# Converting two weight matrices beside the mix steps, and moving the products of zeros behind the first gates

## The chip, the core and the metric

One core of a Trainium2 chip. Its engines are the Tensor engine (PE; its weight loads are shown apart as PEld), the Vector engine (DVE), the Scalar engine (ACT), the GpSimd engine (POOL) and the Sync engine (SP), whose queue issues every transfer of this kernel. The metric is the device time of one execution in microseconds (us). Before the change it is 402.92 us, the median of three runs (402.27 to 406.24).

## What is computed

Three layers in a row on float32 data, 4 batches, 768 positions, 320 channels (8 heads of 40):

```python
# 1. a gated linear recurrence over the positions t, for each head
m_new = max(f[t] + m, i[t]);  f_s = exp(f[t] + m - m_new);  i_s = exp(i[t] - m_new)
C = f_s * C + i_s * outer(v[t], k[t]);  n = f_s * n + i_s * k[t]
x[t] = sigmoid(o[t]) * (C @ q[t]) / max(abs(n . q[t]), 1)
# 2. theta = x @ w_theta; token mixing with two 768 x 768 matrices; a ReLU layer
u = x + w_tok_r @ (x * cos(theta)) + w_tok_i @ (x * sin(theta));  x = u + relu(u @ w_ch)
# 3. a causal convolution of 5 taps (conv_w) as a gate, then two matrices
out = (sigmoid(conv(x)) * (x @ w_val)) @ w_out
```

## The kernel before

The recurrence is computed in blocks, as 12 units of attention (`attend`, L761; four batches, three units of 256 positions each). A unit has a matrix of weights `W` (`weigh`: sums of gate terms in two banks of PSUM, exponentiated by ACT), scores (`scores`: q times k in the same two banks; DVE multiplies them into `W`), the products with v (`numer`, into banks 2 and 3), a carried state (`carry`), the products of q with it (`inter`, into banks 4 and 5), and `finish`, in which DVE reads banks 4, 5, 2 and 3 into `num_m`, divides and writes the result for layer 2. The gates come first (`gates`, L692): scans and exponentials on 32 partitions. `parts` (L707) splits the two rows of gate terms, `G` and `c`, into three bf16 parts each; `weigh` multiplies these.

Layer 2 has 24 steps of mixing (`mix`, L908), six for each pair of batches and half of the positions. A step makes 30 products of 128x128 by 128x384, six into each of the banks 0 to 4. It needs a pair `z` (from `theta`, L824: transposes, products with `w_theta`, sine and cosine) and a pair `w` (from `weight`, L887: in the first twelve steps a token matrix is loaded and converted from 64-bit words, in two buffers `wt_m` used in turn). After six steps `f_u`, `f_ch`, `f_val` and `f_out` (L972 to L1035) do the rest of layers 2 and 3 for that half, between the steps of the next. The banks 0 to 4 are those that attention uses, so the mix begins when the last unit's `finish` has read them.

The small weight matrices come as 64-bit words too. `cv_piece` (L620) loads a third of one (128x320), scales it on ACT (`cv_scale`), puts the bits together with one TENSOR_SCALAR and two SCALAR_TENSOR_TENSOR on DVE (`cv_bits`), copies the high part on ACT and subtracts the low part on DVE or POOL. There are 13 pieces: three each of `w_theta`, `w_ch`, `w_val` and `w_out`, and one of the convolution's weights. They go through two buffers in `xT_m[1]`.

The code does not issue instructions as it runs. Each call is recorded, in program order, by a planner (`Plan`; hence nearly every instruction of the profile has the helper's line, L65), which gives the Tensor engine's steps due times in that order, gives the others the times by which they are needed, and then lists each engine's instructions by its own model of costs. `any2` means DVE or POOL, `copy` means ACT or DVE, as the planner chooses. Each engine then runs its list strictly in order. In the loop below one unit of attention is followed by one piece and by a step (for the negative numbers, of loads, weights and thetas alone):

```python
    for d in range(-1, NG):
        attend(d)
        for piece in [next(todo, None)]:
            if piece:
                cv_piece(*piece)
        step(d - NG)
    stage[0] = 1
    for n in range(NS):
        step(n)
```

At the start, seven products of zeros (`WARM`, L30 and L674) keep the Tensor engine busy while the gates are computed.

Of the kernel before, what the change touches and what calls it, by code (L numbers as in the profile page):

```python
# [7 lines left out]
F32 = mybir.dt.float32  # L8
# [3 lines left out]
I64 = mybir.dt.int64  # L12
# [6 lines left out]
DM = H * D  # L19
# [7 lines left out]
XB = 5  # L27
AHEAD = 3
CVL = (2,)
WARM = 7  # L30
RFIRST = (1,)
GATES = (0, 2, 4)
U = L // 2
NU2 = S // U
FAR = -32768.0
# [35 lines left out]
class Plan:  # L71
# [9 lines left out]
    HOP, TABLE, HOLD = 0.15, 1.3, 5.0  # L81
    WINDOW, PHASE, WARM, COLD = 3.413, 0.6, 0.85, 0.45
    BLOCK, FETCH = 127, 3.6
# [111 lines left out]
    def order(self, aim=None):  # L195
# [27 lines left out]
        def array(n, t):  # L223
# [5 lines left out]
            while todo:  # L229
                some = min(todo, self.BLOCK - used)  # L230
                left = some * each
                while left > 1e-6:
                    w = int((t + self.PHASE + 1e-6) / self.WINDOW)
                    for _ in range(window, w):
                        share, worked = worked / self.WINDOW, 0.0
                        slow = share < (self.WARM if slow else self.COLD)
                    window = w
# [104 lines left out]
def tile_kernel(ctx, tc, qT, kT, kt, v1, og, ig, fg, w_th, w_ch, w_val, w_out, cw, wtok,  # L342
                ident, selL, selR, selG, out):
    plan = Plan(tc.nc)
    act, dve, pool, pe, sp = plan.act, plan.dve, plan.pool, plan.pe, plan.sp
# [42 lines left out]
    k_m = [words(8 * GC * L, f"k_m{i}") for i in range(2)]  # L388
    q_m = words(12 * GC * L, "q_m", place="q")
    xT_m = [words(5 * TH, f"xT_m{i}") for i in range(2)]  # L390
    th_m = words(7 * DM, "th_m")
    num_m = words(2 * TH, "num_m", place="sr")
# [10 lines left out]
    bank = [ps.tile([128, 512], F32, name=f"bank{i}") for i in range(8)]  # L403
# [215 lines left out]

    def cv_piece(nm, src, k_):  # L620
        t = turn("cv", 2)
        raw = xT_m[1][:, t * 2 * DM:(t + 1) * 2 * DM].bitcast(I64)
        v = xT_m[1][:, (4 + t) * DM:(5 + t) * DM]
        if nm == "cw":
            raw, v = raw[:, 0:15], cw_sb.rearrange("p j t -> p (j t)")
        sp.dma_start(out=raw, in_=src if nm == "cw" else src[:, k_ * DM:(k_ + 1) * DM])
        cv_scale(raw, v)
        cv_bits(raw, v)
        if nm == "cw":
            return  # L630
        if nm == "th":
            w0, w1 = (t[:, k_] for t in w_t)
            if k_ == 2:
                pool.memset(w0[64:], 0.0)
                pool.memset(w1[0:64], 0.0)
                dve.tensor_scalar(out=w0[0:64], in0=v[0:64], scalar1=INV2PI, scalar2=None, op0=ALU.mult)
                act.activation(out=w1[64:, 64:], in_=v[64:, 0:256], func=AF.Copy, scale=INV2PI)
                act.activation(out=w1[64:, 0:64], in_=v[64:, 256:], func=AF.Copy, scale=INV2PI)
                return
            dve.tensor_scalar(out=w0, in0=v, scalar1=INV2PI, scalar2=None, op0=ALU.mult)  # L640
            act.activation(out=w1[:, 64:], in_=w0[:, 0:256], func=AF.Copy)
            act.activation(out=w1[:, 0:64], in_=w0[:, 256:], func=AF.Copy)
            return
        hi, lo = wsp[nm]
        act.activation(out=hi[:, k_, 0:DM], in_=v, func=AF.Copy)
        n = DM if nm == "out" else 256
        any2.tensor_tensor(out=lo[:, k_], in0=v[:, 0:n], in1=hi[:, k_, 0:n].bitcast(F32),
                           op=ALU.subtract)
        if n < DM:
            any2.tensor_tensor(out=hi[:, k_, DM:384], in0=v[:, 256:DM],  # L650
                               in1=hi[:, k_, 256:DM].bitcast(F32), op=ALU.subtract)

    pieces = [(nm, src, k_) for nm, src in (("th", w_th), ("ch", w_ch), ("val", w_val),
                                            ("out", w_out)) for k_ in range(3)]
# [11 lines left out]
    G_bf, c_bf = (b_m[:, n * S // 2:(n + 1) * S // 2].bitcast(BF16) for n in range(2))  # L666
# [4 lines left out]
    sp.dma_start(out=i_sb, in_=ig)  # L671
    sp.dma_start(out=id_sb, in_=ident)
    dve.memset(num_m[:, 0:256], 0.0)
    for n in range(WARM):  # L674
        pe.matmul(bank[6 + n % 2][:, 0:256], num_m[:, 0:128], num_m[:, 0:256], start=True, stop=True)
    dve.memset(m_sb[:, 0:1], NEG)
    dve.memset(r_sb, 1.0)
    dve.memset(r_sb.rearrange("p (c l) -> p c l", l=U)[:, :, 0:1], 0.0)
# [13 lines left out]
    def gates(c0, c1):  # L692
        n, a, e = c1 - c0, c0 * L, c1 * L
        m0, m1 = m_sb[:, a:e], m_sb[:, 1 + a:1 + e]
        g, G, c_, w, r, e_ = (t[:, a:e] for t in (g_sb, G_sb, i_sb, w_sb, r_sb, e_sb))
        eng = any2 if c0 else dve
        dve.tensor_tensor_scan(out=m1, data0=f_sb[:, a:e], data1=c_,
                               initial=m_sb[:, a:a + 1] if c0 else NEG, op0=ALU.add, op1=ALU.max)
        eng.tensor_tensor(out=g, in0=f_sb[:, a:e], in1=m0, op=ALU.add)
        eng.tensor_tensor(out=g, in0=g, in1=m1, op=ALU.subtract)  # L700
        dve.tensor_scalar(out=g, in0=g, scalar1=GMIN, scalar2=None, op0=ALU.max)
        if c0 == 0:
            dve.memset(g_sb[:, 0:1], 0.0)
        dve.tensor_tensor_scan(out=G, data0=r, data1=g, initial=0.0, op0=ALU.mult, op1=ALU.add)
        d, mid = d_sb[:, 0:e - a], mid_sb[:, 0:e - a]

        def parts(src, out):  # L707
            copy.copy(out[0:BH, a:e], src)
            eng.tensor_tensor(out=d, in0=src, in1=out[0:BH, a:e], op=ALU.subtract)
            copy.copy(mid, d)  # L710
            copy.copy(out[BH:2 * BH, a:e], mid)
            eng.tensor_tensor(out=d, in0=d, in1=mid, op=ALU.subtract)
            copy.copy(out[2 * BH:3 * BH, a:e], d)

        eng.tensor_tensor(out=c_, in0=c_, in1=m1, op=ALU.subtract)
        eng.tensor_tensor(out=c_, in0=c_, in1=G, op=ALU.subtract)
        parts(G, G_bf)
        parts(c_, c_bf)
        G3, w3, c3 = (t.rearrange("p (c l) -> p c l", l=U) for t in (G, w, c_))
        eng.tensor_tensor(out=w3, in0=c3, in1=G3[:, :, U - 1:U].to_broadcast([BH, 2 * n, U]), op=ALU.add)  # L720
        act.activation(out=w, in_=w, func=AF.Exp)
        e4, G4 = e_.rearrange("p (g u i l) -> p g u i l", i=2, u=2, l=U), G.rearrange(
            "p (g i u l) -> p g u i l", i=2, u=2, l=U)
        for u in range(2):
            act.activation(out=e4[:, :, u], in_=G4[:, :, u], func=AF.Exp)
        tv = bank[5 + turn("g", 3)][:, 0:n * BH].rearrange("p (c h) -> p c h", c=n)
        with plan.joined():
            for c in range(n):
                pe.transpose(tv[:, c, :], w[:, c * L:(c + 1) * L], id_sb[0:BH, 0:BH])
        copy.copy(ew[:, c0:c1, :], tv)  # L730
        tv = bank[5 + turn("g", 3)][:, 0:n * BH].rearrange("p (g u h) -> p g u h", u=2, h=BH)
        with plan.joined():
            for g_ in range(n // 2):
                for u in range(2):
                    o = (2 * g_ + u) * L
                    pe.transpose(tv[:, g_, u], e_[:, o:o + L], id_sb[0:BH, 0:BH])
        copy.copy(ee[:, c0 // 2:c1 // 2], tv)
# [352 lines left out]
            theta(*first_use[n])  # L1090

    parts = []
    todo = iter(pieces)
    for d in range(-1, NG):
        attend(d)
        for piece in [next(todo, None)]:
# [1 line left out]
                cv_piece(*piece)  # L1098
        step(d - NG)
    stage[0] = 1  # L1100
    for n in range(NS):
        step(n)
    stage[0] = 2

    parts.append(part[:])
# [83 lines left out]
```

## Time and profile before

| | |
|---|---|
| median of three runs | 402.92 us (402.27 to 406.24) |
| the profiled execution | 401.29 us, of which 399.6 us are the span from the first to the last instruction |
| PE busy | 359.5 us (90% of the span), mean granted clock 0.936 |
| DVE busy | 324.9 us (81%) |
| ACT busy | 222.0 us (56%) |
| POOL busy | 82.8 us (21%) |

A busy PE is not one at its peak, since products are pipelined. The granted clock is a share of full speed: 0.5 is 1.2 GHz and 1.0 is 2.4 GHz. Engines run side by side, so an engine's idle time matters only where the chain of waits runs through it. "issue" in a wait is time for which the profile shows no reason.

### The profile page before, as it was taken

Reading aid. Unit: us, or ns where it says so; the run is one execution under the profiler, and the core shown is the slowest. Engines: PE = TensorE matmul, PEld = TensorE weight load, DVE = VectorE, ACT = ScalarE, POOL = GpSimd, SP = SyncE. Lnnn points to the kernel's source line nnn. Section 1 sums busy time; section 2 is a strip of 40 time slices with the busy share of each in tenths; the row PEclk is TensorE's granted clock in tenths of the full one; section 3 lists DMA queues with packets and bytes.
Section 4 is the critical chain, followed back from the end, with each engine's and each line's share of the span. In section 5 each row is a group of like instructions: output and inputs, shape, how many; then the busy total and the mean of one; then the engine's idle time right before and its main releaser. Section 6 shows DMA issues by size and latency. Waiting matters only on the chain.

```text
span 399.6 us, 11339 instructions
## 1 busy us (share of the span) xinstructions
PE 359.5 (90%) x4724; PEld 327.0 (82%) x4724; DVE 324.9 (81%) x632; ACT 222.0 (56%) x388; POOL 82.8 (21%) x102
## 2 busy tenths in 40 slices
PE   6877777888969679899999999999999999999996
PEld 4556656576757457799999999999999999999996
DVE  7958977978888899798978998769997759468990
ACT  3562636061866968576534278975697332335563
POOL 7212233345164300000002014023011010213320
PEclk9565889896999878999999999999999999999999
DMA  6977866887788666787875254620410420000204
GB/s 165 292 200 219 270 177 182 226 253 213 201 288 243 180 228 204 243 281 276 287 256 197 100 170 146 214 79 2 157 52 29 157 80 0 2 0 2 99 34 164
DMA packets 29299, 65.62 MB, mean 164 GB/s; under 512 B 5216, under 2 KB 14592, under 8 KB 29248
## 3 DMA queue, kind: packets, MB, share of 16 engines
q1 hardware_dynamic: 29248, 64.90, 51.2%
q8 instruction: 37, 0.61, 0.6%
q14 instruction: 14, 0.11, 0.1%
HBM read 47.58 MB, written 17.30 MB: 162 GB/s over the span
## 4 chain that ended last, share of the span: by engine, by line
PE 71%; DVE 16%; issue 6%; ACT 5%; DMA 1%; SPq 0%; DVEq 0%; ACTq 0%
PE bank L65 71%; DVE k_m L65 5%; DVE th_m L65 2%; ACT th_m L65 2%; DVE r_b L65 2%; DVE xT_m L65 1%; DVE W L65 1%; DVE num_m L65 1%; ACT L65 1%; DVE g_m L65 1%; DVE z L65 1%; DMA g_m<-in_ig_dram 1%; DVE wt_m L65 0%; ACT xT_m L65 0%; ACT xs_hi L65 0%
## 5 line engine op out<-in xcount | busy, mean ns | idle before, releaser
L65 PE MATMUL bank<-wt_m,z 128*128 128x384 f32 x480 | 89.1, 342 | 4.1 <-DVE num_m L65 2.8
L65 PEld LDWEIGHTS bank<-wt_m,z 128*128 128x128 f32 x480 | 83.9, 190 | 5.9 <-ACT xT_m L65 3.1
L65 PE MATMUL bank<-w_r,z 128*128 128x384 f32 x240 | 43.2, 337 | 0.0
L65 PEld LDWEIGHTS bank<-w_r,z 128*128 128x128 f32 x240 | 41.5, 188 | 0.0
L65 DVE SCALAR_TENSOR_TENSOR k_m<-k_m,cw_sb,k_m 128x384 f32<-128x384 f32 (+1 forms) x52 | 40.3, 811 | 0.4
L65 ACT ACTIVATE W<-bank 128x512 f32<-128x512 f32 x24 | 14.2, 597 | 31.5 <-PE bank L65 31.3
L65 POOL TENSOR_TENSOR hl_f<-k_m,hl_f 128x768 fp32r<-128x768 f32 x4 | 8.3, 2083 | 97.1 <-ACT hl_f L65 97.1
L65 ACT ACT_TABLE_LOAD x21 | 26.9, 1283 | 1.4 <-DVE th_m L65 1.0
L65 ACT ACTIVATE th_m<-bank,magic 128x320 f32<-128x320 f32 x24 | 12.6, 524 | 23.1 <-PE bank L65 15.1
L65 DVE TENSOR_TENSOR f_m<-f_m,bank 104x164 f32<-104x164 f32 (+1 forms) x36 | 15.1, 420 | 12.4 <-PE bank L65 8.3
L65 PE MATMUL bank<-r_b,W 64*64 64x41 f32 x768 | 16.8, 242 | 8.5 <-issue 5.5
L65 PE MATMUL bank<-w_t,xT_m 128*128 128x320 f32 x72 | 23.6, 480 | 0.3 <-ACT xT_m L65 0.3
L65 DVE TENSOR_TENSOR k_m<-k_m,bank 104x164 f32<-104x164 f32 (+1 forms) x36 | 15.0, 420 | 10.8 <-PE bank L65 10.7
L65 PE MATMUL bank<-q_m,k_m 64*64 64x64 f32 x768 | 18.3, 237 | 5.9 <-issue 5.2
L65 PE MATMUL bank<-r_b,kw_m 64*64 64x41 f32 (+1 forms) x704 | 18.7, 230 | 5.4 <-issue 2.8
L65 DVE SCALAR_TENSOR_TENSOR r_b<-r_b,r_b 128x768 int32<-128x768 int32 x24 | 22.8, 954 | 0.4
L65 PEld LDWEIGHTS bank<-r_b,W 64*64 64x64 f32 x768 | 14.7, 149 | 10.2 <-issue 6.2
L65 ACT ACTIVATE th_m<-th_m 128x640 f32<-128x640 f32 (+1 forms) x27 | 19.0, 704 | 5.7 <-DVE th_m L65 5.0
L65 PEld LDWEIGHTS bank<-r_b,kw_m 64*64 64x64 f32 (+1 forms) x704 | 15.9, 138 | 7.0 <-issue 3.2
L65 PEld LDWEIGHTS bank<-q_m,k_m 64*64 64x64 f32 x768 | 15.7, 148 | 7.1 <-issue 6.0
L65 POOL TENSOR_TENSOR kw_m<-r_b,ewc 128x320 f32<-128x320 f32 x18 | 13.0, 723 | 40.7 <-PE bank L65 34.5
L65 PEld LDWEIGHTS bank<-w_t,xT_m 128*128 128x128 f32 x72 | 14.9, 213 | 6.8 <-issue 1.6
(213 smaller groups left out, 894.6 us busy)
## 6 DMA issues: line engine op xcount, KB each, us to landing
r_b<-in_wtok_dram SPq DMA_DIRECT2D x24, 384.0 KB
wt_dr<-wt_m SPq DMA_DIRECT2D x12, 768.0 KB
w_r<-wt_dr SPq DMA_DIRECT2D x8, 768.0 KB
r_b<-in_v_dram SPq DMA_DIRECT2D x12, 328.0 KB
q_m<-in_qT_dram SPq DMA_DIRECT2D x24, 160.0 KB
k_m<-in_kT_dram SPq DMA_DIRECT2D x24, 160.0 KB
r_b<-in_kt_dram SPq DMA_DIRECT2D x12, 320.0 KB
x_b<-in_og_dram SPq DMA_DIRECT2D x24, 160.0 KB
```

The source lines that it names most:

```text
L65: calls[u] = lambda e=e: getattr(e, op)(*args, **kw)
```

## The change

`w_val` and `w_out` (`LATER`) leave the loop over the units. Their six pieces are recorded one behind each of the steps 0 to 5 of the mix, and go through two buffers in `k_m[1]`, which holds keys and states of the attention until its end and takes the convolution after step 7. The seven products at the beginning become `WARM = (0, 2, 2)`: none at the beginning, two behind the parts of `G` and two behind the parts of `c` in the first call of `gates`. Those four multiply zeros (`num_m`) with the parts just written, so they wait for them.

```diff
-WARM = 7
+WARM = (0, 2, 2)
+LATER = ("val", "out")
@@ cv_piece
-        raw = xT_m[1][:, t * 2 * DM:(t + 1) * 2 * DM].bitcast(I64)
-        v = xT_m[1][:, (4 + t) * DM:(5 + t) * DM]
+        m = k_m[1] if nm in LATER else xT_m[1]
+        raw = m[:, t * 2 * DM:(t + 1) * 2 * DM].bitcast(I64)
+        v = m[:, (4 + t) * DM:(5 + t) * DM]
@@ the beginning
-    for n in range(WARM):
-        pe.matmul(bank[6 + n % 2][:, 0:256], num_m[:, 0:128], num_m[:, 0:256], start=True, stop=True)
+    def warm(n_, by):
+        for n in range(n_):
+            pe.matmul(bank[6 + n % 2][:, 0:256], num_m[:, 0:128],
+                      by[:, 0:128].unsqueeze(1).to_broadcast([128, 2, 128]), start=True, stop=True)
+    warm(WARM[0], num_m)
@@ gates
-        parts(G, G_bf)
-        parts(c_, c_bf)
+        for src, to, n_ in ((G, G_bf, WARM[1]), (c_, c_bf, WARM[2])):
+            parts(src, to)
+            if c0 == 0:
+                warm(n_, to.bitcast(F32))
@@ the loops
-    todo = iter(pieces)
+    todo = iter([p for p in pieces if p[0] not in LATER])
...
     stage[0] = 1
+    todo = iter([p for p in pieces if p[0] in LATER])
     for n in range(NS):
         step(n)
+        for piece in [next(todo, None)]:
+            if piece:
+                cv_piece(*piece)
```

Since the planner lists everything anew, other instructions move too. Three places follow. The names are the tiles: `bank_97` to `bank_104` are the banks 0 to 7, `xT_m_87` holds a piece of a weight matrix while it is converted before the change, and `k_m_84` after it.

First the Vector engine's list at the end of the attention. These rows come shortly behind the last unit's product of `W` with its scores and end with the reads of banks 4, 5, 2 and 3 by the last `finish`. Before:

```order
L65 TENSOR_SCALAR xT_m_87<-xT_m_87 128x320
L65 SCALAR_TENSOR_TENSOR xT_m_87<-xT_m_87 128x320 x4
L65 SCALAR_TENSOR_TENSOR th_m<-th_m,bank_97 128x320
L65 TENSOR_TENSOR out_lo<-xT_m_87,out_hi 128x320 x2
L65 TENSOR_TENSOR num_m<-bank_101,ewc 128x8x41
L65 SCALAR_TENSOR_TENSOR r_b_82<-r_b_81,r_b_82 128x768
L65 SCALAR_TENSOR_TENSOR th_m<-th_m,bank_98 128x320
L65 TENSOR_TENSOR num_m<-bank_102,ewc 128x8x41
L65 SCALAR_TENSOR_TENSOR r_b_82<-r_b_81,r_b_82 128x768
L65 TENSOR_TENSOR num_m<-num_m,bank_99 128x328
L65 TENSOR_TENSOR num_m<-num_m,bank_100 128x328
```

And after:

```order
L66 RECIPROCAL num_m<-num_m 128x16
L66 SCALAR_TENSOR_TENSOR xT_m_87<-xT_m_87 128x320
L66 TENSOR_TENSOR x_b<-x_b,num_m 128x640
L66 SCALAR_TENSOR_TENSOR xT_m_87<-xT_m_87 128x320
L66 TENSOR_TENSOR x_b<-x_b,num_m 128x640
L66 SCALAR_TENSOR_TENSOR th_m<-th_m,bank_97 128x320
L66 TENSOR_TENSOR num_m<-bank_101,ewc 128x8x41
L66 TENSOR_TENSOR num_m<-bank_102,ewc 128x8x41
L66 TENSOR_TENSOR num_m<-num_m,bank_99 128x328
L66 SCALAR_TENSOR_TENSOR th_m<-th_m,bank_98 128x320
L66 TENSOR_TENSOR num_m<-num_m,bank_100 128x328
```

The pieces of `w_out` are gone, those left on `xT_m_87` are of `w_ch`, and two steps of the conversion of a token matrix (`r_b`) stand elsewhere. From that product of `W` to the last of the four reads there were 28 instructions and are 13.

Then the same engine between step 5 and step 6 of the mix, where `f_u` reads the banks 0 to 4 into `xT_m_86`, and `wt_m_105` receives the low part of step 6's weights. Before:

```order
L65 SCALAR_TENSOR_TENSOR r_b_82<-r_b_81,r_b_82 128x768 x2
L65 TENSOR_TENSOR wt_m_105<-r_b_82,wt_m_105 128x768
L65 TENSOR_TENSOR xT_m_86<-xT_m_86,bank_97 128x384
L65 TENSOR_TENSOR xT_m_86<-xT_m_86,bank_98 128x384
L65 TENSOR_TENSOR xT_m_86<-xT_m_86,bank_99 128x384
```

And after:

```order
L66 TENSOR_TENSOR xT_m_86<-xT_m_86,bank_98 128x384
L66 TENSOR_SCALAR r_b_82<-r_b_82 128x768
L66 TENSOR_TENSOR xT_m_86<-xT_m_86,bank_99 128x384
L66 SCALAR_TENSOR_TENSOR r_b_82<-r_b_81,r_b_82 128x768
L66 TENSOR_TENSOR xT_m_86<-xT_m_86,bank_100 128x384
L66 TENSOR_TENSOR xT_m_86<-xT_m_86,bank_101 128x384
L66 TENSOR_TENSOR wt_m_105<-r_b_82,wt_m_105 128x768
```

Step 6's weights were ready ahead of `f_u`; now they stand behind its last read, that of bank 4.

Last the Tensor engine at the start, up to the first product of `weigh`. Before, from the last of the seven products of zeros on:

```order
L65 MATMUL bank_103<-num_m 128x256
L65 MATMUL bank_102<-id_sb,th_m 128x32 x2
L65 MATMUL bank_103<-id_sb,g_m 128x32 x2
L65 MATMUL bank_104<-th_m 128x64
L65 MATMUL bank_103<-id_sb,g_m 128x32 x2
L65 LDWEIGHTS k_m_83
L65 MATMUL bank_97<-k_m_83 128x512
```

And after, from its first product on:

```order
L66 MATMUL bank_103<-b_m,num_m 128x256
L66 MATMUL bank_104<-b_m,num_m 128x256
L66 MATMUL bank_102<-id_sb,th_m 128x32 x2
L66 MATMUL bank_103<-b_m,num_m 128x256
L66 MATMUL bank_104<-b_m,num_m 128x256
L66 MATMUL bank_103<-id_sb,g_m 128x32 x2
L66 MATMUL bank_104<-th_m 128x64
L66 LDWEIGHTS k_m_83
L66 MATMUL bank_97<-k_m_83 128x512
```

The third and fourth product read the parts of `c` (in `b_m`), which the first unit's `weigh` needs too, and stand ahead of it.

## Rows read from the trace of the kernel before

**Rows 1.** The page's second part: the granted clock in 40 slices.
```profile
PEclk9565889896999878999999999999999999999999
```

**Rows 2.** The chain of waits: start us, us, what. The late pieces.
```profile
149.25 0.41 DVE num_m L65
...
161.93 0.41 DVE th_m L65
162.38 51.21 PE bank L65 x282
...
288.91 107.46 PE bank L65 x641
```

**Rows 3.** Stretches: length, busy time (instructions) of each engine, PE clock, DMA.
```profile
139.30:149.80 10.50, 7.54 (x74) 5.44 (x75) 10.50 (x24) 6.83 (x14) 0.00 (x0) 0.75 0.66 216
149.80:162.40 12.60, 10.83 (x46) 8.44 (x46) 12.38 (x22) 8.22 (x13) 0.00 (x0) 0.86 0.69 228
162.40:193.30 30.90, 30.90 (x167) 28.96 (x168) 26.39 (x36) 21.12 (x31) 0.00 (x0) 1.00 0.78 271
```

**Rows 4.** Groups on DVE, 139.3 to 162.4 us: busy, mean ns, idle before.
```profile
L65 DVE TENSOR_TENSOR x_b<-x_b,num_m 128x640 f32<-128x640 f32 x3 | 2.4, 813 | 0.0
L65 DVE SCALAR_TENSOR_TENSOR xT_m<-xT_m 128x320 int32<-128x320 int32 x5 | 2.1, 468 | 0.0
L65 DVE TENSOR_TENSOR wt_m<-r_b,wt_m 128x768 fp32r<-128x768 f32 x2 | 1.9, 952 | 0.2 <-ACT wt_m L65 0.2
...
L65 DVE SCALAR_TENSOR_TENSOR th_m<-th_m,bank 128x320 f32<-128x320 f32 x3 | 1.4, 478 | 0.0
L65 DVE TENSOR_TENSOR out_lo<-xT_m,out_hi 128x320 fp32r<-128x320 f32 x3 | 1.4, 478 | 0.0
L65 DVE TENSOR_TENSOR num_m<-bank,ewc 128x328 f32<-128x328 f32 x2 | 1.0, 490 | 0.0
L65 DVE TENSOR_TENSOR num_m<-num_m,bank 128x328 f32<-128x328 f32 x2 | 0.9, 489 | 0.0
...
L65 DVE TENSOR_SCALAR xT_m<-xT_m 128x320 int32<-128x320 int32 x2 | 0.6, 313 | 0.0
```

**Rows 5.** DVE in order of time: start us, us, what; last product of W, last bank read.
```profile
138.64 0.67 DVE L65 TENSOR_TENSOR W<-W,bank 128x512 f32<-128x512 f32 x1
...
152.12 0.90 DVE L65 TENSOR_TENSOR num_m<-num_m,bank 128x328 f32<-128x328 f32 x2
```

**Rows 6.** PE in order of time: the mix begins.
```profile
138.77 2.33 PE L65 MATMUL bank<-r_b,W 64*64 64x41 f32 x64 [2.61 <-DVE W L65]
...
149.81 1.29 PE L65 MATMUL bank<-wt_m,z 128*128 128x384 f32 x6 [2.64 <-DVE num_m L65]
...
156.57 3.50 PE L65 MATMUL bank<-w_t,xT_m 128*128 128x320 f32 x12
...
162.38 1.33 PE L65 MATMUL bank<-wt_m,z 128*128 128x384 f32 x6 [1.27 <-DVE th_m L65]
```

**Rows 7.** PE, and ACT ahead of `weigh`, in order of time at the start.
```profile
2.08 6.21 PE L65 MATMUL bank<-num_m 128*128 128x256 f32 x14 [2.08 <-DVE halfpi L65]
...
12.98 0.41 ACT L62 ACTIVATE b_m<-th_m 32x256 bf16<-32x256 f32 x1
...
13.36 0.61 PE L65 MATMUL bank<-k_m 128*128 128x512 bf16 x1
...
21.54 0.44 PE L65 MATMUL bank<-k_m 128*128 128x512 bf16 x1
```

**Rows 8.** Stretches at the start: length, PE busy (instructions), clock, DMA.
```profile
11.00:11.50 0.50, 0.00 (x0) 0.94 1.04 413
...
21.50:22.00 0.50, 0.50 (x7) 0.82 0.63 236
```

**Rows 9.** DVE and POOL in order of time, side by side at 136 us.
```profile
135.90 2.23 DVE L65 SCALAR_TENSOR_TENSOR xT_m<-xT_m 128x320 int32<-128x320 int32 x2
136.12 1.65 POOL L65 TENSOR_TENSOR z<-th_m,z 128x640 fp32r<-128x640 f32 x1 [4.27 <-ACT z L65]
```

## The prediction

> **What bounds the kernel now.** I read the page's strip of the clock first [rows 1]: full speed from about 160 us on, several slices (10 us each) below it before. The chain of waits then splits the run in two [rows 2]. From 162.38 us the Tensor engine's own work makes nearly all of it, in pieces of 51 and 107 us. Ahead of that, the chain runs through the Vector engine at the end of the attention: it is on `num_m` at 149.25 and on `th_m` at 161.93. The table of stretches shows the same [rows 3]: DVE is busy for all of 10.5 us and for 12.38 of the next 12.6, while PE is idle there for 3.0 and 1.8 us and has a clock of 0.75 and 0.86; from 162.4 PE is never idle at 1.0. So up to 162.4 us what counts is how soon DVE frees the banks for the mix, and behind it each us by which PE waits is a us of the run.
>
> The places are in the order of time [rows 5, 6]. DVE finishes the last product of `W` at 139.31 (138.64 + 0.67). PE waited 2.61 us for its first half. The last read of banks 4, 5, 2 and 3 ends at 153.02, so 13.7 us later. The first six products of the mix start at 149.81, those into bank 0 at 162.38, each behind a wait for DVE.
>
> **A. The mix begins sooner: -7.5 us.** The six pieces cost DVE 12 x 0.468 + 6 x 0.313 + 3 x 0.478 = 8.9 us, without the value pieces' few subtractions [rows 4]; most of it stood where DVE had no idle time. By the order, 28 instructions from that product of `W` to the last bank read become 13: three of 0.468 on `w_ch`, two of `x_b` of 0.813, two of `th_m` of 0.478, four bank reads of 0.49 and two small ones of 0.2. Together they are 6.3 us, a little less as they overlap, against 13.7. I followed both lists from the product of `W` (time 0). Before: mix into bank 4 at 10.5, a theta's 3.5 us of products, bank 0 at 23.1. After: numerators to 1.3 (at full clock), a theta to 5, bank 4 at 5, banks 2 and 3 at 6.6 and 8.3, the next theta from 10.6, since ACT has a table, two sines and two scalings ahead of the transposes' copy, bank 0 at about 15.4. The 27 instructions of DVE up to the read that frees bank 0 (46 before) fit in: 14.7 to 16.9 us by [rows 4]. That gives -7.7; the bounds are -6.2 (16.9) and -8.4 (14.7). I take -7.5.
>
> **B. The last units: -1 us.** Up to that product of `W`, DVE loses ten SCALAR_TENSOR_TENSOR and four TENSOR_SCALAR on pieces, 5.9 us by [rows 4], and gets two of `r_b`, three of `x_b` and some of the state in return, so about -2 net. The attention is paced by PE as well, so between 0 and -2.6 (PE's wait for `W` in [rows 6]); I take -1.
>
> **C. The start: +1 us.** The seven products ran from 2.08 for 6.21 us, so 0.89 each [rows 7]. The clock fell to 0.5 at 11.4 us, before the first useful product, and came back at 21.7 [rows 8]. So they hide nothing and warm nothing: taking them away costs nothing. Two new ones wait for `G` and lie in idle time of PE. The other two wait for the last part of `c`, which ACT wrote until 13.39, and `weigh` started behind it at 13.36 and 13.45. Queued behind them on PE are two transposes, a product for `dec`, `weigh` and all scores. They delay these by 2 x 0.89 = 1.8 us, or half of that if the clock is up; DVE and ACT use it for the second gates. If they bring the clock back sooner, a 512-column product takes 0.44 instead of 0.61 [rows 7], and the 8.3 us of work between 13.36 and 21.7 could shrink by 2 to 3. So -2 to +1.8; I take +1, nearer to the delay, since the products are two and a gap of PE lies ahead of them.
>
> The Trainium skill, "TensorE: Matmul & The Clock Gate", section "What's actually happening", says that the slow clock is the default and that activity releases it. By that rule a core without any products up to 10 us would start slow, and speak against this change. The trace agrees in that the clock rose for the seven, but [rows 8] has it low again at 11.4, so by the row the loss is nil.
>
> **D. The mix with the pieces in it: +1.5 us.** From bank 0's first product to `f_u` PE needs 30.9 us, and DVE was busy for 26.4 of them [rows 3]. The pieces add four TENSOR_SCALAR, seven SCALAR_TENSOR_TENSOR and four subtractions, while other work has gone ahead: the list's 52 instructions there (33 before) come to 29 or 30 us. It just fits. On ACT two scalings and two copies a piece, 0.9 us, fit in 9.8 us of idle time. What does not fit is the order of step 6: its weights' low part, 0.952 [rows 4], now stands behind the read of bank 4, about 0.5, and PE has only bank 0's first product to do meanwhile: a stall of some 1.5 us. If DVE runs late there it is more, up to 4. Later weights stand early enough. The six loads go through SP's queue, where the token matrices and `x_dr` are behind them; the first two wait until the last scores have read `k_m[1]`, the third and fourth until a buffer is converted, some 15 us ahead of the need of what is behind them: nothing.
>
> **E. POOL: +0.8 us.** POOL was idle from 139.3 to 193.3 us [rows 3]; now it makes step 0's subtraction of 768 columns beside DVE. At 136 us two DVE instructions took 2.23 us beside one of 1.65 on POOL [rows 9], instead of twice 0.47, so up to 1.3 for one. Bounds 0 and 2.
>
> The Trainium skill, "SBUF — State Buffer", section "Who interferes with whom", has it that these two share a port as an exclusive lock. By that rule the whole of POOL's two instructions could be added, and the sum would be some 2 us higher; the pair in [rows 9] agrees.
>
> **The sum.** -7.5 - 1 + 1 + 1.5 + 0.8 = -5.2 us. The profiled span of 399.6 becomes 394.4, its execution (401.29, so 1.7 outside the span) 396.1. The median of the runs shown is 1.6 above the profiled execution, so I predict **397.5 us**.
>
> **Rivals.** *The gain is taken back.* The mix begins sooner but DVE, at 97% up to `f_u`, falls behind: each token matrix that is late stalls PE, and the clock may drop in such gaps, as in the stretches of 0.75 and 0.86. With 3 us more at D and the start at its upper end the sum is -1.5: 401. For it: [rows 3]. Against it: DVE waited in the old list for the two buffers of `wt_m`, so idle time is there to be filled.
>
> *Slower: the clock of the attention.* The first unit is 1.8 us late, and the clock, low from 10 to 40 us [rows 1], stays low for more of the slices that were at 0.8 to 1.0. The product that took 0.44 us at full took 0.61 at half [rows 7], 1.4 times; at that ratio 10 us of such work are 4 us longer. With the rest as above, and C at its upper bound, one slice gives 402.3 and two give 406.3. It decides from the second on. For it: the 3.9 us between the three runs shown, whose cause I can't see. Against it: the list of PE between 20 and 130 us is nearly the old one.
>
> *A larger gain.* The clock comes back at the start (C at -2) and the last units follow DVE (B at -2.6): -9.8, so 393.
>
> **How the numbers follow.** Forecast (394.5 to 399.5) 0.52, gain taken back (399.5 to 404) 0.21, slower (over 404) 0.10, larger (under 394.5) 0.17. The range of 391.5 to 404 takes the bounds of C and D and leaves out the slower case and the far end of the larger gain, 0.08. About 1% (4 us) is what a measurement of this kernel can tell from no change: faster than 398.9 has the larger gain and most of the forecast, 0.62; slower than 406.9 the worst of the slower case, 0.07; the rest 0.31.
>
> **What would show it.** A: DVE's last bank read some 6 us behind the last product of `W` instead of 13.7, and bank 0's first product 15 to 16 us behind it instead of 23. B: that product at 137 to 139 us. C: the first `weigh` at 15 to 15.7 us and where the clock returns. D: a wait of PE for `wt_m` of 1 to 2 us between steps 5 and 6, and no other before `f_ch`. E: DVE instructions beside POOL's at twice their time. The prediction is wrong if PE has gaps of several us between 20 and 130 us, or waits for `wt_m` in each step.

## The result, and the profile after

| | before | changed |
|---|---|---|
| median (22 executions each) | 402.04 us (398.36 to 407.55) | 404.32 us (400.72 to 410.14) |
| ratio to before, 95% interval | | 1.0061 (1.0033 to 1.0090) |
| profiled executions | 401.29 us (span 399.6) | 408.45 us (406.7); a second one, run later, 401.09 us (399.4) |
| PE, DVE, ACT busy | 359.5, 324.9, 222.0 us | 353.1, 324.9, 221.9 us (second trace) |

The change makes the kernel 0.6% slower, 2.3 us; 397.5 was predicted. Single executions of either kernel scatter by some 9 us, so medians and ratios carry what follows, and one trace shows only where an execution spent its time. Ratios go by the executions within 1.5% of the fastest of their kernel and medians by all, so the two can differ, by 0.6% at the most here. The first trace of the changed kernel is 4 us over its median; rows below are of the second where not said otherwise.

The page's strip of the granted clock, second trace (its 40 slices are those of [rows 1]):

```profile
PEclk9996989898979899999899999999999999999999
```

It is low in 6 slices ahead of 160 us, before in 10; the first two slices can't be read so (see the last section), but from 25 to 134 us too the mean granted clock is 0.88 in this trace (0.84 in the first one) and 0.86 before.

Products on PE at the start, in order of time (start us, us, engine, operation; in brackets the idle time before and what ended it). They answer [rows 7]:

```profile
10.88 2.05 PE L66 MATMUL bank<-b_m,num_m 128*128 128x256 f32 x4 [10.88 <-DVE b_m L64]
...
13.81 2.07 PE L66 MATMUL bank<-b_m,num_m 128*128 128x256 f32 x4 [0.54 <-ACT b_m L63]
...
16.64 0.61 PE L66 MATMUL bank<-k_m 128*128 128x512 bf16 x1
...
22.46 0.38 PE L66 MATMUL bank<-k_m 128*128 128x512 bf16 x1 [0.42 <-DVE W L66]
```

The first `weigh` starts at 16.64 (16.94 in the first trace) instead of 13.36. Two products of zeros take 2.05 us, 1.03 each.

DVE at the end of the attention, answering [rows 5], and below it POOL at the same time:

```profile
138.57 1.27 DVE L66 TENSOR_TENSOR W<-W,bank 128x512 f32<-128x512 f32 x2
139.76 1.80 DVE L66 TENSOR_TENSOR num_m<-num_m 128x16 f32<-128x16 f32 x1
...
147.13 0.49 DVE L66 TENSOR_TENSOR num_m<-num_m,bank 128x328 f32<-128x328 f32 x1
```

```profile
139.70 1.82 POOL L66 TENSOR_TENSOR wt_m<-r_b,wt_m 128x768 fp32r<-128x768 f32 x1 [1.43 <-ACT wt_m L66]
```

The last product of `W` ends at 139.84, the last bank read at 147.62: 7.8 us behind it, 13.7 before. PE there, answering [rows 6]:

```profile
140.16 1.14 PE L66 MATMUL bank<-r_b,W 64*64 64x41 f32 x64
...
145.74 1.31 PE L66 MATMUL bank<-wt_m,z 128*128 128x384 f32 x6 [1.01 <-DVE num_m L66]
...
151.93 3.50 PE L66 MATMUL bank<-w_t,xT_m 128*128 128x320 f32 x12 [1.69 <-ACT xT_m L66]
155.03 4.58 PE L66 MATMUL bank<-wt_m,z 128*128 128x384 f32 x24
...
192.61 3.68 PE L66 MATMUL bank<-wt_m,z 128*128 128x384 f32 x13 [1.89 <-DVE wt_m L66]
```

Bank 0's first product comes at 155.03, 15.2 us behind `W` (23.1 before), and between steps 5 and 6 PE waits 1.89 us for `wt_m`. The table of stretches, answering [rows 3] and [rows 8] (length; busy time and instructions of PE, PEld, DVE, ACT, POOL; granted clock; DMA share; GB/s):

```profile
16.50:17.00 0.50, 0.50 (x2) 0.15 (x3) 0.35 (x3) 0.37 (x1) 0.00 (x0) 1.00 1.08 248
...
140.00:150.00 10.00, 8.99 (x104) 7.19 (x104) 9.86 (x18) 7.83 (x15) 4.40 (x5) 1.00 0.83 276
150.00:160.00 10.00, 8.31 (x41) 6.96 (x40) 10.00 (x18) 8.85 (x15) 0.00 (x0) 1.00 0.84 285
160.00:193.00 33.00, 31.11 (x169) 29.02 (x168) 32.73 (x55) 23.25 (x37) 3.68 (x2) 1.00 0.82 289
```

From 140 to 193 us DVE is idle for 0.4 us in all. The wait of 1.69 us for `xT_m` comes by way of ACT: its scalings of two pieces of `w_val`, 0.5 us each, stand ahead of the sines of a theta, and before the second ACT stops for that piece's load, issued at 139.73 us (the chain of waits; below it ACT in order of time):

```profile
139.73 7.39 DMA k_m<-in_w_val_dram
```

```profile
147.14 0.51 ACT L66 ACTIVATE k_m<-k_m 128x320 f32<-128x320 f32 x1 [0.74 <-DMA k_m<-in_w_val_dram]
147.67 1.28 ACT L66 ACT_TABLE_LOAD   x1
148.96 1.51 ACT L66 ACTIVATE th_m<-th_m 128x640 f32<-128x640 f32 x2
```

In the first trace ACT stops there for 2.01 us, and PE's wait for `xT_m` is 2.3 us. In after_no_zeros, a kernel of the next section with the same list, ACT doesn't stop there, and the wait is 1.4 us. Finally what PE waited for from the last product of `W` on, up to 290 us (us in total, times, longest). Before:

```profile
PE bank L65 <- DVE num_m L65: 3.1, 3, 2.6
PE bank L65 <- DVE th_m L65: 2.0, 3, 1.3
PE bank L65 <- ACT xT_m L65: 0.3, 1, 0.3
```

Changed:

```profile
PE bank L66 <- DVE wt_m L66: 1.9, 1, 1.9
PE bank L66 <- ACT xT_m L66: 1.7, 1, 1.7
PE bank L66 <- DVE k_m L66: 1.4, 1, 1.4
PE bank L66 <- DVE num_m L66: 1.0, 1, 1.0
PE bank L66 <- DVE th_m L66: 0.5, 1, 0.5
PE bank L66 <- ACT k_m L66: 0.4, 1, 0.4
```

The waits that the change was to remove went down (3.1 to 1.0), and others came: 5.4 us in all before, 6.9 after. From the last product of `W` to PE's last product it is 257.0 us before and 256.3 after (257.7 in the first trace). So PE waits 1.5 us more and is busy for 2.2 us less, with a mean granted clock of 0.99 in this stretch instead of 0.98. Almost nothing was gained there in all, and about 3 us were lost ahead of it (1.6 with the first trace's stretch), by subtraction from the medians' 2.3.

### The profile page after: what moved, and what is told of

It is laid out like the page before. It is cut to its first block, busy times and chain, and to the rows that moved or that the text cites. A ratio compares the mean times of both kernels' runs of the same rounds, so it can differ in the third digit from the quotient of the medians.

```text
span 406.7 us, 11324 instructions
## 1 busy us (share of the span) xinstructions
PE 356.9 (88%) x4718; PEld 323.7 (80%) x4718; DVE 324.5 (80%) x636; ACT 221.9 (55%) x391; POOL 80.4 (20%) x94
## 4 chain that ended last, share of the span: by engine, by line
PE 51%; DVE 6%; ACT 5%; issue 1%; ACTq 0%; DVEq 0%
PE bank L66 51%; ACT th_m L66 2%; DVE k_m L66 1%; DVE th_m L66 1%; ACT xs_hi L66 1%; ACT xT_m L66 1%; DVE r_b L66 1%; DVE z L66 1%; DVE sr_f L66 1%; DVE x_b L66 0%; ACT hl_f L66 0%; DVE num_m L66 0%; DVE wt_m L66 0%; ACT L66 0%; DVE xs_hi L66 0%
## 5 line engine op out<-in xcount | busy, mean ns | idle before, releaser
L66 PE MATMUL bank<-wt_m,z 128*128 128x384 f32 x480 | 87.9, 339 | 2.3 <-DVE wt_m L66 1.9
L66 PEld LDWEIGHTS bank<-wt_m,z 128*128 128x128 f32 x480 | 83.0, 188 | 3.8 <-DVE wt_m L66 2.4
L66 PE MATMUL bank<-r_b,kw_m 64*64 64x41 f32 (+1 forms) x704 | 20.5, 239 | 4.6 <-DVE k_m L66 2.3
L66 PE MATMUL bank<-w_t,xT_m 128*128 128x320 f32 x72 | 22.5, 466 | 2.3 <-ACT xT_m L66 2.3
L66 PE MATMUL bank<-r_b,W 64*64 64x41 f32 x768 | 17.9, 248 | 5.7 <-issue 5.1
L66 PEld LDWEIGHTS bank<-r_b,kw_m 64*64 64x64 f32 (+1 forms) x704 | 17.4, 147 | 6.8 <-DVE k_m L66 2.8
L66 PEld LDWEIGHTS bank<-r_b,W 64*64 64x64 f32 x768 | 15.9, 155 | 7.4 <-issue 5.6
L66 ACT ACTIVATE f_m<-bank 64x384 f32<-64x384 f32 x16 | 7.8, 486 | 24.5 <-PE bank L66 24.3
L66 DVE TENSOR_TENSOR x_b<-x_b,num_m 128x640 f32<-128x640 f32 x23 | 20.1, 876 | 1.3 <-ACT x_b L66 1.1
L66 ACT ACTIVATE k_m<-k_m 128x384 f32<-128x384 f32 (+2 forms) x22 | 11.7, 570 | 16.7 <-DVE k_m L66 11.2
```

What stands on the lines that cost most here:

```text
L66: calls[u] = lambda e=e: getattr(e, op)(*args, **kw)
```

## The experiments

All medians, with that of the kernel before taken beside it on the same chip. "Behind W" is the stretch from the last product of `W` to PE's last product in the kernel's one trace. The last column is an estimate: the difference of the medians less that of the stretches behind W, so what the attention lost or gained. The two traces of the changed kernel differ by 1.4 us behind W, so the last column is no surer than that.

| kernel | median | before | ratio (95%) | behind W | ahead, by subtraction |
|---|---|---|---|---|---|
| before | | 402.0 | | 257.0 | |
| changed | 404.3 | 402.0 | 1.0061 (1.0033 to 1.0090) | 256.3 | +3.0 |
| before_no_pieces | 396.3 | 402.0 | 0.9871 (0.9821 to 0.9921) | 256.1 | -4.8 |
| pieces_by_hand | 400.1 | 401.0 | 0.9979 (0.9942 to 1.0016) | 259.8 | -3.7 |
| after_no_pieces | 402.9 | 401.0 | 1.0052 (1.0013 to 1.0092) | 254.7 | +4.3 |
| pieces_alone | 406.5 | 402.0 | 1.0131 (1.0067 to 1.0194) | 257.2 | +4.4 |
| before_four_zeros | 401.7 | 402.0 | 0.9988 (0.9936 to 1.0040) | 257.0 | -0.2 |
| after_no_zeros | 402.3 | 402.0 | none given | 253.6 | +3.7 |
| relisted_fetch | 409.7 | 401.0 | 1.0226 (1.0168 to 1.0284) | 261.8 | +4.0 |
| relisted_hop | 406.6 | 401.0 | 1.0136 (1.0079 to 1.0194) | 262.5 | +0.2 |
| relisted_fetch_up | 409.9 | 402.4 | 1.0128 (1.0057 to 1.0198) | 260.9 | +3.6 |
| after_relisted_fetch | 400.7 | 402.4 | 0.9974 (0.9921 to 1.0026) | 256.4 | -1.1 |
| after_relisted_hop | 407.4 | 402.4 | 1.0121 (1.0052 to 1.0190) | 255.5 | +6.5 |
| after_relisted_up | 409.8 | 402.4 | 1.0211 (1.0152 to 1.0270) | 254.3 | +10.2 |
| joined_lists | 400.8 | 400.9 | 1.0038 (0.9988 to 1.0088) | 258.1 | -1.2 |
| joined_four_zeros | 400.3 | 400.9 | 1.0049 (0.9980 to 1.0117) | 258.0 | -1.6 |
| changed_again | 403.6 | 400.9 | 1.0124 (1.0046 to 1.0202) | 256.3 | +3.4 |
| joined_at_unit_10 | 398.8 | 400.9 | 0.9990 (0.9940 to 1.0040) | 255.0 | -0.1 |
| joined_at_unit_6 | 400.3 | 400.9 | 1.0005 (0.9964 to 1.0046) | 256.5 | -0.1 |

**The pieces, with the lists held.** In these kernels the planner's list is made as in the kernel before (or the changed one), and only when it is issued are steps left out or put in. So nothing else moves. In the two kernels without pieces the load, the scaling and the bits (three instructions of DVE) of each of the six are left out; the copies of the high parts and the subtractions stay where they were. In pieces_by_hand the whole pieces move.

```diff
 before_no_pieces, after_no_pieces
         for n in best[1]:
+            if n in self.skip:      # load, scaling and bits of w_val and w_out
+                continue
 pieces_by_hand: besides, behind given products of the mix
+            for call in at.get(n, []):
+                call()              # load; scaling; bits; high part and subtraction
```

before_no_pieces:

> The kernel before with its lists as they are, but the six pieces of w_val and w_out are neither loaded nor put together (their high parts and subtractions work on what lies in the buffer), so the output is made with wrong matrices. It shows what the pieces cost where they stood, with nothing given back in the mix. My prediction's steps A and B: 7.5 and 1 us, so 393 to 395, the first product of the mix into bank 0 at 154 to 156 us instead of 162.4. Rival: the end of the attention is paced by PE and by ACT, and DVE's time there is not passed on: 399 to 402.

pieces_by_hand:

> The kernel before with its lists as they are; only the six pieces of w_val and w_out are taken out of them and set by hand between the products of the steps 0 to 7 of the mix, in the same two buffers of k_m[1] as in the change, with their subtractions on POOL. Nothing else moves, the seven products of zeros stay. Leaving the pieces out of these lists gave 396.3 us against 402.0. Theory L, the lists: the change loses because the planner lists the attention anew and worse, not because of what the pieces cost in the mix; then this kernel keeps most of the 5.7 us: 397 to 399. Theory P, the pieces in the mix: DVE has no room there and the gain is taken back: 401 to 404, with waits of PE for wt_m or f_u of 4 us in all.

after_no_pieces:

> The changed kernel with its lists as they are, but the six pieces of w_val and w_out are neither loaded nor put together where they now stand, in the mix (the output is made with wrong matrices). The same work as the kernel before without its pieces (396.3 us), in the other lists. Theory L, the lists: still some 4 to 6 us over that, 400 to 402.5. Theory P, the pieces in the mix: 396 to 397.5, so 7 us under the changed kernel's 404.3.

Leaving that work out of the old list is worth 5.7 us (396.3, between the two ranges), most of it ahead of the last product of `W`, not behind it as A said: behind it only 0.9. There the chain of waits now goes through two loads of a token matrix (start us, us, what), so it is not DVE's work alone that paces the end of the attention:

```profile
131.21 2.98 DMA r_b<-in_wtok_dram
...
139.60 3.63 DMA r_b<-in_wtok_dram
```

Putting the pieces into the mix by hand gives 3.7 us back behind `W` (259.8 against 256.1), and 4.8 by the medians, each against its own kernel before. The stretch from 157 to 209 us shows how. Without pieces:

```profile
157.00:209.00 52.00, 52.00 (x289) 50.07 (x289) 43.27 (x63) 30.77 (x45) 1.85 (x1) 1.00 0.75 266
```

With them:

```profile
157.00:209.00 52.00, 49.23 (x266) 45.86 (x265) 49.13 (x73) 33.47 (x54) 9.25 (x9) 1.00 0.73 253
```

PE was busy for all of 52.00 us and is idle for 2.8 with the pieces, DVE goes from 43.3 to 49.1 and POOL from 1.9 to 9.3. PE's waits in it:

```profile
PE bank L65 <- DVE wt_m L65: 1.7, 2, 1.2
PE bank L65 <- DVE th_m L65: 1.3, 1, 1.3
PE bank L65 <- DVE k_m L65: 1.1, 1, 1.1
PE bank L65 <- DVE xT_m L65: 0.4, 1, 0.4
```

(The 1.3 for `th_m` ends ahead of 157 us and is there without the pieces too.) So theory P is right in part. But after_no_pieces decides for theory L: the changed lists, with that work of the six pieces left out, are still 0.5% slower than the kernel before, and by medians 6.6 us over the same work in the old lists (7.6 with each less its own kernel before).

It shows one thing more. In the changed lists the pieces cost little: against the changed kernel the medians, each less its own kernel before, differ by 0.3 us, the stretches behind `W` by 1.6 (3.0 with the first trace). What goes with them is the wait behind ACT's scalings (PE's for `xT_m` falls from 1.7 to 0.2). The other waits of the mix stay, 1.77 us for `wt_m` between steps 5 and 6, 1.41 and 0.39 for `k_m`, though DVE is busy for 30.2 of the 33 us from 160 on instead of 32.7. So these come with the order, not with DVE's load. PE's waits behind `W` in after_no_pieces:

```profile
PE bank L66 <- DVE wt_m L66: 1.8, 1, 1.8
PE bank L66 <- DVE k_m L66: 1.4, 1, 1.4
PE bank L66 <- ACT xT_m L66: 0.2, 1, 0.2
```

**The pieces moved, the start as before**, with lists made anew (`WARM = (7, 0, 0)`):

> The changed kernel with the seven products of zeros at the beginning as before and none behind the parts; all lists are made anew. Theory 1, the start: the first weigh at 13.5 us, and what the moved pieces gain at the end of the attention (4.9 us in the changed kernel's profile, less some 2 lost between steps 5 and 6) shows: 399.5 to 401. Theory 2, the new lists: as the changed kernel, 403.5 to 405.

1.3% over before, though its first `weigh` starts at 11.8 us. So a loss comes without the new start too, if in yet another list, and theory 1 fails here.

**The start.** In before_four_zeros the lists of before are held, and the four products stand for the seven (their second pair writes zeros over transposed gate terms in two banks before they are read, so what follows is computed from zeros). In after_no_zeros the changed lists are held and the four left out.

> The kernel before with its lists as they are; the seven products of zeros at the beginning are left out, and two stand behind the parts of G and two behind those of c, as in the change. Theory 1, the start: 3 us over the kernel before, 404.5 to 405.5, the first weigh at 16 to 17 us. Theory 2, the new lists: no difference, 401.5 to 402.5.

> The changed kernel with its lists as they are, only the four products of zeros left out (they write what nobody reads). In the changed kernel's profile the first weigh starts at 16.94 us (13.36 before). Theory 1, the start: those four products cost 3 us there and the attention carries the delay to its end; then the first weigh comes at 14 to 14.5 us and the time is about 3 us under the changed kernel's 404.3: 401 to 402. Theory 2, the new lists: the attention is late because of where its instructions now stand, whatever the start; then the time stays at 403.5 to 405.

With the four products the first `weigh` came at 16.84 in the old lists, and the time is the same (0.9988). There the delay is not passed on: at the first unit the product of `W` ends at 24.57 in this trace and at 21.09 in that of before, at the second at 35.66 and 37.27. For the changed lists it is not settled. Without the four they gave 402.3, and all six executions lie at or under 402.94, as do 9 of the 28 of the changed kernel; against its own kernel before that is 0.3 us more, where the changed kernel has 2.3. In its one trace the last product of `W` ends no sooner (140.09, and 139.84 in the second trace of the changed kernel), though the first `weigh` comes at 13.87. So up to 2 us of the loss may be the start's.

**Lists made anew, with nothing else changed.** One number of the planner's model is another (`FETCH` 3.6 to 3.5 or 3.7, or `HOP` 0.15 to 0.16), in the kernel before and in the changed one.

```diff
-    BLOCK, FETCH = 127, 3.6
+    BLOCK, FETCH = 127, 3.5
```

> The kernel before with one number of the planner's model changed (FETCH 3.6 to 3.5), so that it lists the same instructions in another order; no work is added or taken away. Theory L: the order alone moves the time by several us in either direction, 398 to 408, mostly upwards if the order before was a lucky one. Theory P: nothing, 401 to 403.

> The kernel before with another number of the planner's model changed (HOP 0.15 to 0.16), the same instructions in a third order. Theory L: 398 to 408, and not the same as with the other number. Theory P: 401 to 403.

> The kernel before, listed with FETCH at 3.7 instead of 3.6. Theory L: another draw, 402 to 410, over the 401 to 402 of the list before. Rival C, for which the order says little: 401 to 403.

> The changed kernel, listed with FETCH at 3.5 as the relisted kernel before (409.7 us against 401.0). Theory L, the lists: each new list is a draw that moves the time by several us, and the list before was a good one; the change itself, on lists alike in that, is worth some -2 us (5.7 gained where the pieces were, 3.8 given back in the mix, by the two kernels with the lists held): then this kernel is on the average faster than 409.7, 403 to 408. Rival C, the change itself costs its 2.3 us: 411 to 413.

> The changed kernel, listed with HOP at 0.16 as the relisted kernel before (406.6 us). Theory L: 400 to 406, so under it, and another time than the changed kernel's 404.3. Rival C: 408 to 410.

> The changed kernel, listed with FETCH at 3.7. Theory L: some 2 us under the kernel before with that number, 400 to 408. Rival C: 2 us over it.

The same instructions in another order cost 1.3 to 2.3% in all three cases: the list before is the best of its four by more than 5 us. The trace of relisted_fetch (413.7 us, 4 over its median) shows waits of PE behind `W` that the list before doesn't have:

```profile
PE bank L65 <- ACT wt_m L65: 3.4, 1, 3.4
PE bank L65 <- DVE wt_m L65: 3.2, 1, 3.2
PE bank L65 <- DVE th_m L65: 2.7, 3, 2.2
```

The waits are not all of it. The mean granted clock of the three relisted kernels' executions is 0.92 to 0.93, that of the kernel before beside them 0.94, and the kernel before itself takes longer at a lower clock: beside before_no_pieces its fastest execution, 396.04 us, has 0.961 and its slowest, 407.42 us, 0.920. What of the loss is waiting and what is the clock that went with it, the runs don't separate.

The changed kernel takes 400.7 to 409.8 us in its three other lists. Against the kernel before with the same number (medians, each less its own kernel before) it is 10.5 us faster, 0.7 faster, and level; by the ratios it is 2.5% faster, 0.1% faster, and 0.8% slower, the last within the two intervals. So the second half of theory L, that the change is worth some 2 us in lists drawn alike, is neither shown nor excluded. Rival C, by which it costs 2.3 us in each, misses in two and is open in the third. One thing is steady, by one trace of each: behind `W` the changed lists need 254.3 to 256.4 us and the relisted ones of before 260.9 to 262.5, some 6 less.

**The lists joined.** Both lists are made in one kernel. Up to a given product of `W` each engine follows the old one (without pieces), from there the changed one.

```diff
+        old, new = lists
+        i = max(i for i, (n, u) in enumerate(old) if n in self.wsteps[-2:]) + 1
+        head = [(n, u) for n, u in old[:i] if n not in self.late]
+        done = {n for n, u in head}
+        tail = [(n, u) for n, u in new if n not in done and n not in self.zeros]
```

> The changed kernel on two lists joined: up to the last product of W each engine follows the list of the kernel before (without the six pieces, with the seven products of zeros), from there on the list of the changed kernel, pieces in the mix included. Taking 1.7 us outside the span and the stretch from that product to the end out of the medians, the product stands at 138.5 us in the runs of the list before without pieces, and at 145 to 149 in the changed kernel's. Theory A, the loss is made by the new list of the attention: 138.5 + 1.7 + the 253.6 to 257.7 us that the changed kernel needs from there, so 394 to 398, under both kernels. Theory B, the new list of the mix works only because the attention's list did part of its work ahead, so the loss comes back behind that product: over 258 us from there to the end and 399 to 403 in all.

> The same joined lists with the change's four products of zeros in place of the seven (on two banks that nobody uses then). If the start passes its delay on, 3.5 us over the joined lists with the seven: 397 to 401. If it is absorbed, as with the kernel before, the same within 1 us.

> The changed kernel itself, beside the two joined ones on one chip. Theory A: 403 to 405, so 7 to 10 us over the joined lists; from the last product of W to the end 253.6 to 257.7 us.

> The changed kernel on the two lists joined one unit earlier: the list of the kernel before (without pieces) up to the last product of W of the unit before the last, the changed kernel's list from there. Joined at the last unit it took 400.8 us, with 258.1 us from the last product of W to the end, of which PE waited 2.8 for x_dr; the changed kernel took 403.6 and 256.3. If the loss is made before the last unit, the old list keeps it out and the wait for x_dr goes: 397 to 400. If the last unit's new list makes the loss: 402 to 404.

> The same, joined after the seventh of the twelve units. If the new list loses evenly over the units, half of the 2.8 us between the joined and the changed kernel is back: 400 to 403. If it loses in the second half: 402 to 404.5; if in the first half: 397 to 400.

(The places of the product at 138.5 and 145 to 149 us in the first of these are 3.2 us too late, since PE's last product is not the end of the span; as the same was left out on both sides, the sums stand.) Theory A asked for 394 to 398 and joined_lists took 400.8 with 258.1 us behind `W`, as theory B said: PE waits 2.8 us there for `x_dr`. Joined one unit earlier that wait is gone from there (1.3 us of it stand ahead of `W`), 255.0 us behind `W`, and the median is 398.8. So both had a part. What holds in all four joined kernels is that the old list, in the first seven units alone (400.3) or in more of them, brings the changed kernel from 403.6 to between 398.8 and 400.8. With 400.28, at the edge of two of the ranges above, joined_at_unit_6 has nothing of the loss back over joined_lists (400.76), so most of it is made in the first seven units: by their new list, or by the four zeros in that list, which joined_at_unit_6 doesn't have. joined_at_unit_10 has the lowest median of all kernels that compute everything, 2.1 us under before and 4.8 under the changed kernel; its ratio of 0.9990 doesn't tell it from before. In the old list of the attention the four zeros cost nothing here either (400.3 beside 400.8).

Where in the attention? PE's waits between 17 and 132 us, before:

```profile
PE bank L65 <- issue: 15.6, 12, 2.5
PE bank L65 <- DVE k_m L65: 2.6, 3, 1.3
PE bank L65 <- DVE W L65: 2.5, 4, 0.9
PE bank L65 <- ACT W L65: 0.7, 1, 0.7
PE bank L65 <- DVE f_m L65: 0.2, 1, 0.2
```

Changed (second trace):

```profile
PE bank L66 <- issue: 13.4, 10, 3.3
PE bank L66 <- DVE k_m L66: 3.1, 4, 1.7
PE bank L66 <- DVE W L66: 2.8, 3, 1.3
PE bank L66 <- DVE num_m L66: 2.7, 5, 1.0
PE bank L66 <- DVE f_m L66: 0.5, 2, 0.4
```

joined_lists:

```profile
PE bank L66 <- issue: 15.8, 11, 3.9
PE bank L66 <- DVE W L66: 4.1, 6, 1.1
PE bank L66 <- DVE k_m L66: 2.5, 3, 1.3
PE bank L66 <- DVE th_m L66: 1.4, 2, 1.1
PE bank L66 <- DVE num_m L66: 0.4, 1, 0.4
```

In the new list PE waits five times for `num_m`, the reads that free the banks 2 to 5 for the next unit: 2.7 us, none before, 0.4 where the old list is kept. It is the one large wait that is new there, and about the size of the loss, but these traces don't show it to be the cause. PE is idle for 25.3 us in all from the first `weigh` to the last product of `W` before and for 24.4 in this trace of the changed kernel, since its gaps called issue are shorter; the product ends at 139.3 and 139.8 us (145.8 in the first trace). So this execution hardly shows the loss that the medians have. Joined at unit 10 the wait is 1.9 us in three, with a better time. Which rows of the first seven units make the loss stays open.

## Why the prediction was wrong

Two steps failed: ahead of `W` the list was taken as given (3.0 of the 7.5 us by which the sum missed), behind it A counted how much sooner an instruction comes instead of what PE had to gain, and D left out two waits and put the loads at nothing (the other 4.5).

**Ahead of `W`: the list was taken as given.** Against the slower rival the prediction said that the list of PE between 20 and 130 us is nearly the old one. Up to the last product with `W` it has nearly the same instructions, some 2050, but more than 500 of them stand in another order. The prediction priced three places where rows had moved and the instructions that had gone, and gave the re-ordered rest no price (B -1, C +1). The runs: a new order alone costs 1.3 to 2.3% in three of three cases, and the changed kernel takes 2.8 to 4.8 us more than the joined kernels. The rival "slower" has the measured time in its range (over 404), but by luck: it named the start and a lower clock in the attention. In the old lists the start is absorbed, in the changed ones it may be part of the loss, and the granted clock from 25 us on is no lower on the whole (0.88 and 0.84 beside 0.86).

**Behind `W`: A, right in its places, wrong in its price.** Predicted were the last bank read 6 us and bank 0's first product 15.4 us behind `W`; they came at 7.8 and 15.2. But the 7.7 us between 23.1 and 15.4 were not 7.7 us of the run. In the old list PE had done 24 products of the mix when it came to bank 0, in the new one 18, and six transposes that stood behind the last 64 products with `W` now stand ahead of them. More simply: PE was idle for 2.96 and 1.77 us in the two stretches of [rows 3], 4.7 us in all, so no more than that could be gained there, apart from the clock of 0.75 and 0.86. I had the rows and compared arrivals instead of PE's idle time. What was gained is 3.1 + 1.3 + 0.3 less 1.0 + 1.7, so 2.0 us of waits, and the clock, which is 1.00 there now. The 1.7 is the wait behind the two scalings of `w_val`.

**D, right in its place, too small.** The wait between steps 5 and 6 was put at 1.5 us and is 1.89. "No other before `f_ch`" held; behind it came 1.4 us in `f_val` for the convolution in `k_m` and 0.4 in `f_out`. DVE has no idle time left there (32.73 of 33.00 us busy), but that isn't the cause: after_no_pieces has the same three waits. The prediction's own reason, the place of step 6's low part behind the read of bank 4, holds. What failed is that it had no later wait, and "nothing" for the six loads: ACT stops 0.74 us (2.01 in the first trace) for one of them, ahead of the theta that PE needs next. A had the two scalings there in its list; PE's wait of 1.7 us behind them is 1.4 with the load in time, and 0.2 without load and scalings. Set by hand into the old lists, at other places, the pieces cost 3.7 us in the mix, near the end of the range to 4 that I had given and not taken.

**E, right, twice its size.** POOL's subtraction for `wt_m` (1.82 us) lies beside a DVE instruction of 128x16 that takes 1.80 us; others of that kind take 0.18 (mean of four between 85 and 139 us). So 1.6 us of DVE's time where 0.8 was predicted, within the bounds of 0 and 2; what of it reached the end of the run is not shown. The Trainium skill, "SBUF — State Buffer", section "Who interferes with whom", calls the shared port an exclusive lock; the pair agrees: DVE's small instruction ended when POOL's did.

**B, wrong in its sign.** With the list held, the pieces' going is worth 4.8 us ahead of `W`, beyond the end of -2.6 that I had given; with the list that the change gets, the attention is some 3 us longer by subtraction.

**C, right that the seven hide nothing, wrong in what the four cost.** Predicted 15 to 15.7 us for the first `weigh`, came 16.6 to 16.9: each product took 1.03 us, not 0.89, two transposes and the product for `dec`, 0.8 us, now stand between them and `weigh`, and ACT's last part came 0.4 us later (13.75). In the old list of the attention it cost nothing that shows in the end, by two pairs of kernels (before and before_four_zeros, joined_lists and joined_four_zeros); in the changed list that is open.

**The sum.** Behind `W`: predicted -5.2 (A, D, E), measured -0.7 (+0.7 in the first trace). Ahead of it: predicted 0 (B and C), measured +3.0 by subtraction. Together +2.3. In the second trace A brought some 4.2 us instead of 7.5 (2.0 of waits and, at the most, the 2.2 by which PE is busy for less), and D's waits are 3.7 instead of 1.5. (396.1 and 1.6 make 397.7, not the 397.5 that was said.) Against the relisted kernels of before, the part behind `W` is some -6: there that part of my sum would have been about right, but the list that I compared with was better than the three others that were drawn, which one trace doesn't tell.

## What to carry to other kernels

Where a program makes the order of the instructions, a change draws a new order: price it by what another order of the same instructions costs (change a number of the planner's model a little and look), and hold the old order when you want to know what the change itself does. A stretch can give back no more than the idle time and the slow clock that the engine which sets the end has in it; how much sooner one instruction starts is no gain if other work has moved behind it. Moving work beside an engine that is busy for 26.4 of 30.9 us is a matter of where it is set: six pieces of some 1.25 us each on DVE cost 3.7 us behind `W` by hand, with POOL beside it, and between 0.3 (medians) and 3.0 (single traces) in the places that the planner gave them. And a load isn't free where an engine that keeps a strict order stops for it ahead of work that others need.

## What the runs showed of the hardware

The granted clock is not the clock of the products at the start. In the changed kernel its row says 1.00 at 16.5 us, and the product of 512 columns takes 0.61 us there and at 18.17, as it does in [rows 7] at 13.36, between the clock's fall and its return in [rows 8]; at 22.46 it takes 0.38. So a core that has had no products up to 10.88 us does start slow, and the row shows it only after the clock's first fall. The Trainium skill, "TensorE: Matmul & The Clock Gate", section "What's actually happening", says that the slow state is the default and activity releases it; the durations agree, the row doesn't.

PE has gaps in the attention that end with nothing that the profile shows ("issue"): 8 to 13 of them, up to 5.8 us long (after_no_zeros), 10.5 to 18.6 us in all between the first `weigh` and the last product of `W`. With the same lists and other zeros it was 16.7 us in 13 gaps (before) and 11.8 in 10 (before_four_zeros), and the last product of `W` ended at 139.3 and at 134.3. The gaps are the smaller part of that: from the first `weigh` on PE was busy for 100.3 and 94.2 us, and from 25 to 134 us the granted clock was 0.86 and 0.92. Single executions of one kernel lie as far apart (139.8 and 145.8 in the two traces of the changed kernel); what makes the gaps the runs don't show.
